# Attention with hashed buckets and a squared-ReLU block: the last key block of the softmax sums, and two small operations moved with it

## The chip, the cores and the metric

The kernel runs on one core of one Trainium2 chip. The metric is the device time of one execution in microseconds (us). It was timed three times before the change: 906.41, 908.99 and 909.02, so the median is 908.99 us. The profiled execution is another one; it counted 907.58 us, and its profile spans 905.8 us.

## The reference

There are 4 x 8 heads of 768 tokens and 64 features. Each token gets a 6-bit bucket number from the signs of a small projection, and a query attends only to the keys of its own bucket. The result goes, head by head, side by side, into a two-layer block with a squared ReLU.

```python
q_bits = (np.einsum('bhsd,dk->bhsk', q, proj) > 0)     # and k_bits
mask = q_bucket[:, :, :, None] == k_bucket[:, :, None, :]
scores = np.where(mask, scale * q @ k.T, -1e9)
attn = np.exp(scores - max); attn = attn / (attn.sum(-1, keepdims=True) + 1e-09)
x = attn @ v                                           # to (3072, 512)
h = np.maximum(x @ w_in, 0.0)                          # (3072, 2048)
out = (h * h) @ w_out                                  # (3072, 512)
```

Above, the lines are shortened: `@` stands for the batched products. The part that the change touches is the sum `attn.sum(-1)` of the exponentials over the keys, its reciprocal, and the preparation of the key bits.

## The kernel before, in words

The kernel has two stages. In the first one (up to about 345 us) attention is done for 16 pairs of heads, one turn of the loop over `pr` each; the second one does the two dense layers. The order of all instructions in the first stage is written out by hand: each engine runs its own instructions in the order in which the code issues them, and an instruction waits by semaphores for what it reads and for the buffers that it overwrites.

One turn of the loop over `pr` does these things. The keys are cut into six blocks of 128 (`SB` is 6). `score` (L375) makes the scores of one key block against all 768 queries of both heads, transposed, so that keys lie on the partitions. It does so in two pieces, of 512 and 256 queries, with two kinds of matmul into the same sum (L385). The first multiplies bits (bf16), which adds a huge negative number where the buckets differ; the second multiplies features (fp32). ScalarE takes the exponential (L389) into `e`, one of four ring buffers, which are used in turn. The score tiles take turns in three PSUM slots, which `hash` and `tot` (below) use too.

`attend` (L406) multiplies the exponentials of a key block with the values, into `xo`. The sum over the keys has two parts. Within a partition, `add_up` (L395) has VectorE add the exponentials of one key block after another to `total`, 128 x 1536 numbers each time; it is called for blocks 1 to 4 and starts with blocks 0 and 1 together. Across partitions, and with the sixth block (number 5), `sum_up` (L422) has TensorE multiply both `total` and the sixth block's `e` with a matrix of ones, 128 x 32, into `tot` (L430): for each of the two sources one matmul per head and half of the queries, each into 32 of the 128 partitions of `tot`. The four of one source thus use the four column tiles of TensorE. An fp32 matmul appears as two in the profile, so L430 has sixteen per turn. VectorE then transposes `tot` (`flip`, L436), adds a tiny constant (L438), takes the reciprocal (L442) and spreads it over two halves (`both`, L444). `spread` (L450) has TensorE distribute this over the partitions, and `normalize` (L461) multiplies `xo` with it and stores the result.

Pairs overlap. In turn `pr`, after the first two scores, `finish(pr - 1)` does the hash matmuls for pair `pr + 1` (`prepare`: `hash_bits`, L337, and then `signs` on ScalarE, L347, eight of them), then `sum_up`, the last two `attend` and `spread` of pair `pr - 1`. `features` (L321) transposes queries and keys of the next pair on VectorE. `weigh` (L368) multiplies the key bits of the next pair, 128 x 768 in bf16, by a factor per partition (`gains`); it is a VectorE instruction (L371), issued after the first `add_up` and before `normalize`, and in the first turn after block 3's `add_up`.

Between these the loop prepares the dense layers' weights, which arrive as float64: `load_weight` (L121, on SP's queue), `part_weight` (L134, VectorE, L141 and L145), `place_power` (L151, ScalarE, L158 and L159) and `round_weight` (L161, VectorE, L169 to L177), two pieces a turn. In six turns (pairs 4, 5, 8, 9, 10 and 11; the dictionary `sums`, L510) VectorE also makes sums of weights or of activations at the end of the turn (`sums_in`, L495, and `sums_x`, L534).

## Time and profile before

| | |
|---|---|
| Median of three runs | 908.99 us |
| Span of the profiled execution | 905.8 us |
| VectorE adds L402 | 64, median 1752 ns |
| TensorE L430, both sources | 256 matmuls, medians 498 and 486 ns |
| VectorE factor L371 | 15, median 414 ns |
| VectorE constant L438 | 16, median 173 ns |
| ScalarE exponentials L389 | 192, 591 to 1034 ns |

The page of the profile has the busy time of each engine, the span in 40 slices (here about 22.6 us each), the DMA queues, the chain of waits, and the costliest groups of instructions. The engines are PE (TensorE), PEld (its weight loads), DVE (VectorE), ACT (ScalarE), POOL (GpSimd) and SP (SyncE). The chain of waits is followed back from the last instruction of the execution: at each step to what released it, or to the instruction before it on its engine. The slices show how full the engines are along the span; attention takes the first fifteen.

```profile
PE   8999999999999999999999999999999999999994
...
DVE  5788899798998885887777776677778666777874
ACT  5878878887788761222211112221111122221110
```

A digit is the busy share in tenths; TensorE's row counts as busy also where matmuls overlap each other. In a timeline, a row gives start, length, engine, line, operation, tiles, sizes and count, and in brackets how long the engine was idle before it and what ended that. Since matmuls overlap, the length of a row is not what it moves TensorE on by; the start of the next row tells that.

### The profile page before, as it was taken

How to read it: one execution, taken by the hardware profiler on the slowest of the kernel's cores; microseconds unless marked ns; L12 is line 12 of the kernel's file. 1: busy time of each engine (PE TensorE's matmuls, PEld its weight loads, DVE VectorE, ACT ScalarE, POOL GpSimd, SP SyncE). 2: the span in 40 equal slices, each digit the busy share in tenths (PEclk: the TensorE clock that was granted, in tenths of full speed). 3: DMA queues.
4: the chain of work that ended last, by engine and by line, in shares of the span. 5: the costliest groups of instructions: out<-in, count | busy, mean ns of one | idle time of the engine just before them, and what ended most of it. 6: DMA issues, size and time to landing. Idle time of an engine off the chain costs nothing.

```text
span 905.8 us, 11897 instructions
## 1 busy us (share of the span) xinstructions
PE 884.4 (98%) x4372; PEld 504.5 (56%) x4372; DVE 697.6 (77%) x1012; ACT 363.4 (40%) x593; POOL 91.4 (10%) x149
## 2 busy tenths in 40 slices
PE   8999999999999999999999999999999999999994
PEld 3444444444444444443688854445888644458884
DVE  5788899798998885887777776677778666777874
ACT  5878878887788761222211112221111122221110
POOL 2000000000000000564000011112000211100002
PEclk9999999999999999999999999999999999999998
DMA  9577769778977326999765735557757455545575
GB/s 180 107 146 139 198 175 204 172 251 210 233 182 162 112 99 185 279 273 287 253 219 159 178 67 151 152 151 221 278 150 183 75 151 152 149 130 159 144 188 82
DMA packets 253407, 158.14 MB, mean 175 GB/s; under 512 B 166496, under 2 KB 215648, under 8 KB 253344
## 3 DMA queue, kind: packets, MB, share of 16 engines
q1 hardware_dynamic: 218448, 84.04, 39.4%
q10 hardware_dynamic: 24160, 37.89, 14.4%
q0 software_dynamic: 10736, 35.40, 12.8%
q8 instruction: 36, 0.59, 0.3%
q14 instruction: 27, 0.22, 0.1%
HBM read 119.28 MB, written 38.01 MB: 174 GB/s over the span
## 4 chain that ended last, share of the span: by engine, by line
PE 93%; DMA 3%; DVE 2%; ACT 1%; issue 1%; ACTq 0%; DVEq 0%
PE acc L675 57%; PE st L385 17%; PE xo L412 14%; PE tot L430 3%; PE hash L337 2%; DMA w_unit<-w_in 2%; DMA k_nat<-in_k_dram 1%; ACT bits L347 1%; ACT e L389 0%; DVE peaks L716 0%; DVE b L765 0%; DMA out_dram<-ot 0%; DMA leaf<-w_out 0%; DVE h L764 0%; DVE t L491 0%
## 5 line engine op out<-in xcount | busy, mean ns | idle before, releaser
L389 ACT ACTIVATE e<-st 128x1024 f32<-128x1024 f32 x192 | 145.2, 810 | 67.7 <-PE st L385 62.7
L675 PE MATMUL acc<-x,w_unit 128*128 128x512 f32 x384 | 169.6, 593 | 1.8 <-DMA w_unit<-w_in 1.8
L385 PE MATMUL st<-feat,feat 64*128 64x512 f32 (+1 forms) x768 | 150.4, 483 | 0.0
L412 PE MATMUL xo<-e,v_nat 128*64 128x512 f32 (+1 forms) x768 | 134.8, 492 | 0.0
L675 PE MATMUL acc<-b,leaf 128*128 128x256 f32 x600 | 133.0, 379 | 0.0
L675 PE MATMUL acc<-t_x,w_unit 128*128 128x512 f32 x288 | 127.8, 593 | 0.0
L675 PEld LDWEIGHTS acc<-x,w_unit 128*128 128x128 f32 x384 | 72.8, 190 | 92.7 <-issue 89.2
L675 PEld LDWEIGHTS acc<-b,leaf 128*128 128x128 f32 x600 | 113.8, 190 | 17.1 <-issue 1.7
L412 PEld LDWEIGHTS xo<-e,v_nat 128*64 128x64 f32 x768 | 51.4, 136 | 82.4 <-issue 70.3
L675 PEld LDWEIGHTS acc<-t_x,w_unit 128*128 128x128 f32 x288 | 54.5, 190 | 69.8 <-issue 67.7
L385 PEld LDWEIGHTS st<-feat,feat 64*128 64x128 f32 x768 | 66.1, 188 | 34.9 <-issue 26.8
L402 DVE TENSOR_TENSOR total<-total,e 128x1536 f32<-128x1536 f32 x48 | 84.2, 1753 | 1.7
L764 DVE TENSOR_TENSOR h<-acc,two 128x512 f32<-128x512 f32 x24 | 16.6, 691 | 86.2 <-PE acc L675 86.2
L675 PE MATMUL acc<-t,leaf 128*128 128x256 f32 x336 | 76.6, 380 | 0.8 <-ACT one L682 0.4
L682 ACT COPY two<-acc 128x512 f32<-128x512 f32 (+1 forms) x45 | 21.9, 486 | 131.8 <-PE acc L675 113.3
L347 ACT ACTIVATE bits<-hash,lifts 32x384 bf16<-32x384 f32 x124 | 70.9, 572 | 7.1 <-issue 3.5
L675 PEld LDWEIGHTS acc<-t,leaf 128*128 128x128 f32 x336 | 63.6, 190 | 10.5 <-DVE t L491 1.1
L682 ACT COPY one<-acc 128x512 f32<-128x512 f32 (+1 forms) x45 | 21.9, 486 | 117.0 <-PE acc L675 75.2
L765 DVE SCALAR_TENSOR_TENSOR b<-h 128x512 f32<-128x512 f32 x96 | 64.2, 690 | 2.5
L385 PE MATMUL st<-bits,bits 64*128 64x256 bf16 (+1 forms) x384 | 63.2, 325 | 2.4 <-ACT e L389 1.2
L675 PE MATMUL acc<-b_t,leaf 128*128 128x256 f32 x240 | 54.2, 380 | 1.3 <-issue 1.3
L675 PEld LDWEIGHTS acc<-b_t,leaf 128*128 128x128 f32 x240 | 45.4, 190 | 8.1 <-issue 2.0
(125 smaller groups left out, 871.4 us busy)
## 6 DMA issues: line engine op xcount, KB each, us to landing
leaf<-w_out ACTq DMA_DIRECT2D x142, 256.0 KB, 3.0
w_unit<-w_in SPq DMA_DIRECT2D x24, 896.0 KB, 6.0
raw<-in_moe_w_in_dram SPq DMA_DIRECT2D x16, 512.0 KB, 5.5
raw<-in_moe_w_out_dram SPq DMA_DIRECT2D x16, 512.0 KB, 4.7
w_out<-sums POOLq DMA_DIRECT2D x16, 448.0 KB, 7.0
v_nat<-in_v_dram SPq DMA_DIRECT2D x16, 384.0 KB, 4.9
x_all<-x_t SPq DMA_DIRECT2D x16, 384.0 KB, 3.1
x<-x_all POOLq DMA_DIRECT2D x3, 2048.0 KB, 13.0
```

The source lines that it names most:

```text
L337: nc.tensor.matmul(out=banks[g * NR_B:(g + 1) * NR_B, h, 0:HS], lhsT=projs[rows], rhs=feat[pr, w][rows, c * HS:(c + 1) * HS], start=True, ...
L347: nc.scalar.activation(out=t[h * D:h * D + NR_B, c * HS:(c + 1) * HS], in_=hashed[pr, w][at, h, 0:HS], func=ACTF.Sign, scale=HUGE, bias=li ...
L385: nc.tensor.matmul(out=st[:, h, 0:hi - lo], lhsT=src[pr, 1][rows, key], rhs=src[pr, 0][rows, lo:hi], start=first, stop=not first,)
L389: nc.scalar.activation(out=e[:, :, lo:hi], in_=st[:, :, 0:hi - lo], func=ACTF.Exp, scale=scale)
L402: nc.vector.tensor_tensor(out=totals[pr], in0=in0, in1=weights[pr, kt][:, :, 0:S], op=ALU.add)
L412: nc.tensor.matmul(out=xo[h * D:(h + 1) * D, lo:hi], lhsT=nat[pr, "v_nat"][:, h, kt * D:(kt + 1) * D], rhs=weights[pr, kt][:, h, lo:hi], s ...
L430: nc.tensor.matmul(out=tot[g * 32:(g + 1) * 32, 0:HS], lhsT=ones, rhs=src[:, h, c * HS:(c + 1) * HS], start=src is totals[pr], stop=src is ...
L675: nc.tensor.matmul(out=acc[to], lhsT=a(i), rhs=b(i), start=first and i == 0, stop=last and i == n - 1, skip_group_check=True,)
L682: nc.scalar.copy(out=t, in_=acc[of])
L764: nc.vector.tensor_tensor(out=h, in0=one, in1=two, op=ALU.add)
L765: nc.vector.scalar_tensor_tensor(out=out[:, r], in0=h, scalar=0.0, in1=h, op0=ALU.max, op1=ALU.mult)
```

## The change

It has five parts, all in the first stage.

- `add_up` is also called for the sixth key block (number 5), at the end of the turn, in the ten turns whose pair is not in `sums`. In those, `sum_up` multiplies only `total` with the ones; in the other six pairs it still multiplies both sources.
- The first add of a pair becomes an operation with a scalar, which adds the tiny constant `SB * TINY` to the sum of blocks 0 and 1 on each partition.
- For that, the add of the constant `S * TINY` after the flip (L438) goes; the reciprocal reads the flip itself.
- `weigh` becomes a ScalarE activation (Copy with a factor per partition) in place of the VectorE multiplication.
- `weigh` is issued elsewhere: after the scores of blocks 2 and 3 and ahead of `place_power(a)`, and in the first turn after the scores of blocks 4 and 5 and ahead of `place_power(b)`.

```diff
     def weigh(pr):
 
         t = bits[pr, 1]
-        nc.vector.tensor_scalar(out=t, in0=t, scalar1=gains, scalar2=None, op0=ALU.mult)
+        nc.scalar.activation(out=t, in_=t, func=ACTF.Copy, scale=gains)
...
     def add_up(pr, kt):
 
-        if kt == 0 or kt == SB - 1:
-            return
         if kt == 1:
             totals[pr] = p_n.tile([P, 2, S], FP32, name="total")
-        in0 = weights[pr, 0][:, :, 0:S] if kt == 1 else totals[pr]
-        nc.vector.tensor_tensor(
-            out=totals[pr], in0=in0, in1=weights[pr, kt][:, :, 0:S], op=ALU.add
-        )
+            nc.vector.scalar_tensor_tensor(
+                out=totals[pr], in0=weights[pr, 0][:, :, 0:S], scalar=SB * TINY,
+                in1=weights[pr, 1][:, :, 0:S], op0=ALU.add, op1=ALU.add,
+            )
+        else:
+            nc.vector.tensor_tensor(
+                out=totals[pr], in0=totals[pr], in1=weights[pr, kt][:, :, 0:S], op=ALU.add
+            )
...
         tot = tot[:, 0]
-        for src in (totals[pr], weights[pr, SB - 1]):
+        srcs = [totals[pr]] + [weights[pr, SB - 1]] * (pr in sums)
+        for src in srcs:
             for c in range(2):
                 for h in range(2):
                     g = 2 * h + c
                     nc.tensor.matmul(
                         out=tot[g * 32:(g + 1) * 32, 0:HS], lhsT=ones,
                         rhs=src[:, h, c * HS:(c + 1) * HS],
-                        start=src is totals[pr], stop=src is not totals[pr],
+                        start=src is srcs[0], stop=src is srcs[-1],
                     )
         flip = p_n.tile([P, HS], FP32, name="flip")
         nc.vector.transpose(out=flip, in_=tot[:, 0:HS])
         once = p_n.tile([P, NB], FP32, name="once")
-        nc.vector.tensor_scalar(
-            out=once, in0=flip.rearrange("p (n f) -> p n f", f=32)[:, :, 0],
-            scalar1=S * TINY, scalar2=None, op0=ALU.add,
+        nc.vector.reciprocal(
+            out=once, in_=flip.rearrange("p (n f) -> p n f", f=32)[:, :, 0]
         )
-        nc.vector.reciprocal(out=once, in_=once)
...
-            elif more:
-                weigh(pr + 1)
             if pr > 0:
                 normalize(pr - 1)
...
             if pr == 0:
                 prepare()
+            elif more:
+                weigh(pr + 1)
             place_power(a)
...
-            if pr == 0:
-                weigh(1)
...
             score(pr, 5)
+            if pr == 0:
+                weigh(1)
             place_power(b)
             attend(pr, 2)
             attend(pr, 3)
             add_up(pr, 4)
+
+            if pr not in sums:
+                add_up(pr, 5)
             if pr in sums:
```

## The prediction

> **What bounds the kernel now.** I read the page first (engines, then the chain of waits), to see whose work sets the end.

> ```profile
> PE 884.4 (98%) x4372; PEld 504.5 (56%) x4372; DVE 697.6 (77%) x1012; ACT 363.4 (40%) x593; POOL 91.4 (10%) x149
> ...
> PE 93%; DMA 3%; DVE 2%; ACT 1%; issue 1%; ACTq 0%; DVEq 0%
> PE acc L675 57%; PE st L385 17%; PE xo L412 14%; PE tot L430 3%; PE hash L337 2%; DMA w_unit<-w_in 2%; DMA k_nat<-in_k_dram 1%; ACT bits L347 1%; ACT e L389 0%; DVE peaks L716 0%; DVE b L765 0%; DMA out_dram<-ot 0%; DMA leaf<-w_out 0%; DVE h L764 0%; DVE t L491 0%
> ```

> TensorE holds 93% of the chain, in the attention (up to about 345 us) as in the dense part. The change touches attention alone, and of the chain there only `tot L430`. So what matters is whether TensorE can really start the next thing earlier once half of L430 is gone. For that I took the timeline of the turn that starts at 113.9 us.

> ```profile
> 117.24 0.88 PE L337 MATMUL hash<-feat,projs 64*32 64x384 f32 x16
> ...
> 118.05 0.85 PE L430 MATMUL tot<-total,ones 128*32 128x384 f32 x8
> ...
> 118.36 4.68 ACT L347 ACTIVATE bits<-hash,lifts 32x384 bf16<-32x384 f32 x8
> ...
> 118.72 0.83 PE L430 MATMUL tot<-e,ones 128*32 128x384 f32 x8
> ...
> 119.47 2.81 PE L412 MATMUL xo<-e,v_nat 128*64 128x512 f32 x16
> ...
> 119.61 0.58 DVE L436 STREAM_TRANSPOSE flip<-tot 128x384 f32<-128x384 f32 x1 [0.69 <-PE tot L430]
> ...
> 120.23 0.17 DVE L438 TENSOR_SCALAR once<-flip 128x12 f32<-128x12 f32 x1
> ...
> 122.47 0.41 DVE L371 TENSOR_SCALAR bits<-bits,gains 128x768 bf16<-128x768 bf16 x1
> ...
> 123.92 0.38 PE L385 MATMUL st<-bits,bits 64*128 64x512 bf16 x2
> ...
> 126.75 0.72 ACT L158 ACTIVATE small<-power,excess 128x512 uint8<-128x512 uint32 x1
> ...
> 127.50 0.63 ACT L159 ACTIVATE power<-small 128x512 uint32<-128x512 uint8 x1
> ...
> 129.67 3.13 ACT L389 ACTIVATE e<-st 128x1024 f32<-128x1024 f32 x4 [1.54 <-PE st L385]
> ```

> TensorE goes from one row to the next without a hole; VectorE and ScalarE wait for it (0.69 and 1.54 us). The first `tot` start of one turn lies 20.55 us before that of the next in nearly every turn. The windows tell how full the two others are, one turn without weight sums (60 to 81 us) and one with them (101 to 122):

> ```profile
> 60.00:81.00 21.00, 21.00 (x162) 9.68 (x160) 17.47 (x24) 16.68 (x26) 0.00 (x0) 1.00 0.66 126
> ...
> 101.00:122.00 21.00, 21.00 (x162) 9.64 (x160) 19.96 (x28) 16.68 (x26) 0.00 (x0) 1.00 0.62 160
> ```

> Columns: PE, PEld, DVE and ACT busy, with instruction counts. VectorE has 3.5 us free in 21 in the first and 1.0 in the second; ScalarE 4.3 in both. The sums-free turns are the ten that get the sixth add.

> [...] L402 has a median of 1752 ns. [...] in L430 each matmul takes 0.49 us, yet eight of them move TensorE on by only 118.72 - 118.05 = 0.67 us.

> **The change part by part.**

> *Sums on TensorE, removed in ten turns.* Four products of two matmuls each go. They are not worth 8 x 0.49 us but what TensorE moves on: groups of four (one per column tile) start at 118.05, 118.39, 118.72 and 119.05, then the attend at 119.47. The step from the last group to the attend stays; two groups at 0.33 go, 0.66 us. The chain of waits gives 1.43 us for sixteen, 0.71 for half; I take 0.66.

> *The sixth add on VectorE, ten times 1.75 us.* The adds for which it runs are the sums-free pairs 0 to 3, 6, 7 and 12 to 15. It stands after the fifth add and ahead of the next `features` (two transposes, 0.97 and 0.94 us), whose results hash needs, and of `round_weight` (three at 0.69), ahead of the flip. In the turn shown the four sums of the weights stand in that very place, 4 x 0.63 = 2.5 us start to start, and hash was in time (k-features ended 117.02, its second half started about 117.6). 1.75 is less than 2.5, so features and flip come no later than here. VectorE's load in a sums-free turn becomes 17.1 (17.47 x 20.55/21) + 1.75 - 0.41 - 0.17 = 18.3 us of 19.9: hidden, with 1.6 to spare. In the last pair it isn't hidden: its fifth add starts at 337.87, the sixth could start at 339.54 and end at 341.29, where `tot` started at 341.04. That is 0.3 us of delay, and 0.35 of the 0.66 is left.

> *The key factor to ScalarE, 15 times.* Off VectorE: 0.41 us. On ScalarE: the trace has no such row. L158 with 256 elements more, at the 0.85 ns an element between the 512 and 1024 exponentials (593 and 1027 ns), gives 0.94 us[...]. Bounds 0.85 (L159 alike) and 1.0; I take 0.93. It stands after the exponential of block 3 and before L158. Behind it are L158 and L159 and then the exponential at 129.67, and who waits for those is `round_weight` on VectorE and the score slots on TensorE. From 126.75, 0.93 + 1.38 ends at 129.1: under 129.67, so the 1.54 us idle hides it. `round_weight` (128.94 before) comes some 0.2 us late, less than what VectorE has gained by then (0.41 + 0.17). In the first turn the factor stands after the exponential of block 5, which ended at 30.14; ready by about 31.1, needed by the next turn's first score at 31.69. The added wait of ScalarE on its own signs costs nothing, as these are done by then.

> *The constant with the first sum.* Two-tensor operation with a scalar: 0.69 us for 512 elements (L177) against 0.68 for the plain add (L485), so 1.75 again; upper bound 1.85 from L471 (1.02 at 768, reading PSUM). The 0.17 us of L438 go from the path flip, once, spread, which was hidden behind the 2.81 us attend. SP's and POOL's queues keep their order.

> *Sum.* 9 x 0.66 + 0.35 = 6.3 us, from 905.8 (this profile's span) to 899.5. That execution counted 907.58, and the three timed ones 906.41 to 909.02. Off the median of 908.99: 902.7.

> **The rivals.**

> *ScalarE's signs hold TensorE (gain 1.5 to 4 us, 905 to 907.5).* The third score tile of a turn (123.92) takes the PSUM slot of `hash`, free when the eight signs end at 118.36 + 4.68 = 123.04. These follow hash, not `tot`, so they don't move up. TensorE would now ask at 123.26. A release takes about 0.05 us where the trace shows one (signs ended at 25.79, score at 25.84), so 0.17 us is left. For: the margin is thin, and the exponential behind the signs must follow closely. Against: it suffices by these rows. It touches the eight shortened turns that have signs.

> *The gain is given back at a transfer (gain about 2.3 us, 906.7).* In one later turn VectorE waited for weights:

> ```profile
> 215.13 0.43 DVE L141 TENSOR_SCALAR power<-raw 128x512 uint32<-128x512 uint32 x1 [1.96 <-DMA raw<-in_moe_w_out_dram]
> ```

> That turn took 22.41 instead of 20.55 us. Six shortened turns lie before it; were the landing fixed in time, 6 x 0.66 = 4.0 would go. Against: its requests are issued by the same loop after x is stored, and at 184 to 192 us the DMA is nearly idle, so it moves along.

> *Slower: VectorE becomes the bound of the ten turns (912).* If its waits inside a turn (for exponentials, placed powers, `tot`) come to more than the 1.6 us to spare, each turn lags, and the features make hash late. With 1 us lag a turn, nine times 1.0 - 0.66 = +3 us. For: VectorE is at 95% in sums turns. Against: these run at 20.55 with more work on it. It decides only from a sixth add dearer than about 3.3 us.

> **How the numbers follow.** Forecast 0.68, signs 0.13, transfer 0.11, VectorE 0.08. About 0.3% (2.7 us) is what a measurement of this kernel can tell from no change. The forecast is faster but for a few hundredths, two thirds of the signs case and a third of the transfer case too: faster 0.79, same 0.13, slower 0.08. Range: the forecast with the spread of the runs before (906.4 - 6.3 = 900.1, less 0.4 for 0.71 instead of 0.66) gives 899.7 below; above, the signs case down to a gain of 2.6 us, 906.4.

> **What would show it.** Right: `tot` with 176 matmuls instead of 256, 1.75 us adds 74 instead of 64; start to start of `tot` about 19.9 us in the shortened turns; L371 on ScalarE at 0.93 us with no new wait of TensorE. Wrong: TensorE waiting in `st` for `bits L347`, or in hash for `feat`; VectorE no longer waiting at the flip; the wait at the weights of that one turn grown by more than a microsecond; L371 above 1.6 us.

## The result, and the profile after

The changed kernel took 900.88 us (median of six, 899.60 to 905.62), the kernel before beside it 908.04 us (906.41 to 909.02). The ratio is 0.9932, with a 95% interval of 0.9906 to 0.9957: faster by 0.7%, or 7.2 us. The forecast was 902.7 us, a gain of 6.3 from the 908.99 us of the first three runs before; 1 us of the difference between 902.7 and 900.88 is that the kernel before has a median of 908.04 us here.

The profile is of the slowest of these six executions: it counted 905.62 us and spans 903.8. TensorE's granted clock was halved once in its dense stage (0.50 from 412.78 to 419.60 us), which the last section takes up; so the whole span can't be set against the 905.8 before. The attention stage has the full clock in both (1.00). The first matmul of the dense stage starts at 345.29 us before and at 337.62 after: attention lost 7.67 us. A second profile of the changed kernel (run `after_again`, below) has 337.86, in a span of 898.4.

From the page of the changed kernel, engines and the head of the chain of waits:

```profile
PE 880.1 (97%) x4292; PEld 503.7 (56%) x4292; DVE 711.4 (79%) x991; ACT 376.0 (42%) x608; POOL 91.7 (10%) x149
...
PE 88%; DMA 5%; DVE 4%; ACT 1%; issue 1%; ACTq 0%; SPq 0%; DVEq 0%
```

TensorE has 80 matmuls fewer, and VectorE 13.8 us more work. A shortened turn, in the timeline after (the lines that answer to those shown before; L433 is the old L430, L414 the old L412, L439 the old L436; L404 are the adds, of which the second at 88.72 is the sixth, and L324 the features behind it):

```profile
75.00 0.88 PE L337 MATMUL hash<-feat,projs 64*32 64x384 f32 x16
...
75.80 0.85 PE L433 MATMUL tot<-total,ones 128*32 128x384 f32 x8
76.12 4.68 ACT L347 ACTIVATE bits<-hash,lifts 32x384 bf16<-32x384 f32 x8
76.59 2.81 PE L414 MATMUL xo<-e,v_nat 128*64 128x512 f32 x16
76.72 0.58 DVE L439 STREAM_TRANSPOSE flip<-tot 128x384 f32<-128x384 f32 x1 [0.65 <-PE tot L433]
...
81.04 0.38 PE L385 MATMUL st<-bits,bits 64*128 64x512 bf16 x2
...
83.86 0.94 ACT L371 ACTIVATE bits<-bits,gains 128x768 bf16<-128x768 bf16 x1
84.71 0.71 ACT L158 ACTIVATE small<-power,excess 128x512 uint8<-128x512 uint32 x1
85.44 0.63 ACT L159 ACTIVATE power<-small 128x512 uint32<-128x512 uint8 x1
...
86.78 3.13 ACT L389 ACTIVATE e<-st 128x1024 f32<-128x1024 f32 x4 [0.71 <-PE st L385]
...
88.72 3.61 DVE L404 TENSOR_TENSOR total<-total,e 128x1536 f32<-128x1536 f32 x2
...
93.14 0.93 DVE L324 STREAM_TRANSPOSE feat<-k_nat 128x768 f32<-128x768 f32 x1
```

From `tot` to the attend it is now 0.79 us (75.80 to 76.59), where it was 1.42. TensorE waits for nothing here: the features that hash needs end at 94.07 us, and the next hash starts at 94.90. ScalarE, with the factor in its queue, waits 0.71 us for the scores instead of 1.54. VectorE still waits for TensorE at the flip, 0.65 us. The 0.69 us in the turn shown of before are no measure for this, as that turn has weight sums: in the turns without sums VectorE waited 3.2 us there. That wait has paid for the sixth add. All waits at the flip between 40 us and the end of attention, before and after (in total, how often, the longest):

```profile
DVE flip L436 <- PE tot L430: 33.0, 15, 3.2
```

```profile
DVE flip L439 <- PE tot L433: 11.3, 15, 1.6
```

The stretch from 60 to 81 us, which before had 17.47 us of VectorE and 16.68 of ScalarE:

```profile
60.00:81.00 21.00, 21.00 (x158) 9.66 (x156) 19.62 (x24) 18.13 (x28) 0.00 (x0) 1.00 0.69 126
```

The distances between the first `tot` starts of successive turns tell what each turn takes (us; "to 1" is from the `tot` of pair 0 to that of pair 1):

| | to 1, 2, 3, 4 | to 5, 6 | to 7, 8 | to 9 | to 10, 11, 12 | to 13 | to 14 | to 15 | then to the dense stage |
|---|---|---|---|---|---|---|---|---|---|
| before | 20.55 each | 20.55 each | 20.55 each | 22.41 | 20.55 each | 20.55 | 19.75 | 16.41 | 4.25 |
| after | 19.91 each | 20.55 each | 19.91 each | 20.55 | 20.55 each | 19.91 | 19.10 | 16.26 | 3.60 |

Each distance contains the `tot` of the pair that it starts from. Nine of the ten shortened ones give 0.64 or 0.65 us. Pair 14's, in the column "to 15", gives only 0.15, as TensorE has to wait 0.43 us ahead of the last `tot`. The turn "to 9" lost 1.86 us that no part of the change was forecast to touch: the wait for the weights is gone. The start-up takes 0.15 us more (0.39 in `after_again`).

### The profile page after: what moved, and what is told of

Same layout as the page of the kernel before. It is cut to its first block, busy times and chain, and to the rows that moved or that the text cites. A ratio compares the mean times of both kernels' runs of the same rounds, so it can differ in the third digit from the quotient of the medians.

```text
span 903.8 us, 11749 instructions
## 1 busy us (share of the span) xinstructions
PE 880.1 (97%) x4292; PEld 503.7 (56%) x4292; DVE 711.4 (79%) x991; ACT 376.0 (42%) x608; POOL 91.7 (10%) x149
## 4 chain that ended last, share of the span: by engine, by line
PE 88%; DMA 5%; DVE 4%; ACT 1%; issue 1%; ACTq 0%; SPq 0%; DVEq 0%
PE acc L679 54%; PE st L385 17%; PE xo L414 14%; DMA w_unit<-w_in 3%; PE tot L433 2%; PE hash L337 2%; DMA out_dram<-ot 1%; DVE total L404 1%; DMA k_nat<-in_k_dram 1%; ACT bits L347 1%; DVE peaks L720 0%; DVE ot L834 0%; DVE b L769 0%; ACTq L809 0%; ACT e L389 0%
## 5 line engine op out<-in xcount | busy, mean ns | idle before, releaser
L679 PE MATMUL acc<-x,w_unit 128*128 128x512 f32 x384 | 172.2, 600 | 4.2 <-DMA w_unit<-w_in 4.2
L389 ACT ACTIVATE e<-st 128x1024 f32<-128x1024 f32 x192 | 145.2, 810 | 50.1 <-PE st L385 45.6
L385 PE MATMUL st<-feat,feat 64*128 64x512 f32 (+1 forms) x768 | 150.4, 483 | 0.0
L414 PE MATMUL xo<-e,v_nat 128*64 128x512 f32 (+1 forms) x768 | 134.8, 492 | 0.0
L679 PE MATMUL acc<-b,leaf 128*128 128x256 f32 x600 | 132.9, 379 | 0.0
L679 PE MATMUL acc<-t_x,w_unit 128*128 128x512 f32 x288 | 127.8, 593 | 0.5 <-ACT one L686 0.5
L679 PEld LDWEIGHTS acc<-x,w_unit 128*128 128x128 f32 x384 | 73.8, 193 | 96.8 <-issue 90.6
L679 PEld LDWEIGHTS acc<-b,leaf 128*128 128x128 f32 x600 | 114.0, 190 | 16.8 <-issue 1.4
L404 DVE TENSOR_TENSOR total<-total,e 128x1536 f32<-128x1536 f32 x58 | 101.9, 1757 | 3.8
L414 PEld LDWEIGHTS xo<-e,v_nat 128*64 128x64 f32 x768 | 51.3, 136 | 82.4 <-issue 75.0
L679 PEld LDWEIGHTS acc<-t_x,w_unit 128*128 128x128 f32 x288 | 54.5, 190 | 70.2 <-issue 67.7
L385 PEld LDWEIGHTS st<-feat,feat 64*128 64x128 f32 x768 | 66.1, 188 | 33.9 <-issue 25.2
L679 PE MATMUL acc<-t,leaf 128*128 128x256 f32 x336 | 76.6, 380 | 0.7 <-ACT one L686 0.4
L347 ACT ACTIVATE bits<-hash,lifts 32x384 bf16<-32x384 f32 x124 | 71.0, 573 | 4.9 <-PE hash L337 1.6
L679 PEld LDWEIGHTS acc<-t,leaf 128*128 128x128 f32 x336 | 63.6, 190 | 10.5 <-DVE t L492 1.1
L385 PE MATMUL st<-bits,bits 64*128 64x256 bf16 (+1 forms) x384 | 63.2, 325 | 2.4 <-ACT e L389 1.2
L679 PE MATMUL acc<-b_t,leaf 128*128 128x256 f32 x240 | 54.2, 380 | 2.0 <-issue 2.0
L679 PEld LDWEIGHTS acc<-b_t,leaf 128*128 128x128 f32 x240 | 45.4, 190 | 8.8 <-issue 2.7
```

The lines of the kernel that those rows point to most:

```text
L347: nc.scalar.activation(out=t[h * D:h * D + NR_B, c * HS:(c + 1) * HS], in_=hashed[pr, w][at, h, 0:HS], func=ACTF.Sign, scale=HUGE, bias=li ...
L385: nc.tensor.matmul(out=st[:, h, 0:hi - lo], lhsT=src[pr, 1][rows, key], rhs=src[pr, 0][rows, lo:hi], start=first, stop=not first,)
L389: nc.scalar.activation(out=e[:, :, lo:hi], in_=st[:, :, 0:hi - lo], func=ACTF.Exp, scale=scale)
L404: nc.vector.tensor_tensor(out=totals[pr], in0=totals[pr], in1=weights[pr, kt][:, :, 0:S], op=ALU.add)
L414: nc.tensor.matmul(out=xo[h * D:(h + 1) * D, lo:hi], lhsT=nat[pr, "v_nat"][:, h, kt * D:(kt + 1) * D], rhs=weights[pr, kt][:, h, lo:hi], s ...
L679: nc.tensor.matmul(out=acc[to], lhsT=a(i), rhs=b(i), start=first and i == 0, stop=last and i == n - 1, skip_group_check=True,)
```

## The experiments

**Which part does what.** Two kernels with one half of the change each. `sixth_only` leaves the factor and the constant as they were before:

```diff
-        if kt == 0 or kt == SB - 1:
+        if kt == 0:
             return
...
-        for src in (totals[pr], weights[pr, SB - 1]):
+        srcs = [totals[pr]] + [weights[pr, SB - 1]] * (pr in sums)
+        for src in srcs:
...
             add_up(pr, 4)
+            if pr not in sums:
+                add_up(pr, 5)
```

> Only the sixth add of the ten pairs and the dropped second source; the key factor stays on VectorE in its old place and the small constant stays after the flip. My theory (TensorE moves up by what it no longer does, VectorE has room): the shortened turns take 19.9 us, attention loses 6.2 us, and the whole is 902 us beside 908. If the stall of 1.9 us in the turn after the weight wait is tied to how early x is stored, it stays here. Rival (VectorE needs the relief by the two small moves): without it the features make hash late in the shortened turns, TensorE waits there for VectorE, and less than half of the gain, under 3 us, is left (905 or more).

Measured: 900.83 us (six executions, 898.42 to 903.54), ratio 0.9933 (0.9913 to 0.9953). Shortened turns 19.91 us, the turn "to 9" 21.72, and attention ends at 338.99. The rival falls: VectorE keeps up without the relief. By the times, the sixth add alone gives the whole gain (900.83 and 900.88 us); what the small moves add to it shows in the traces alone. `small_only` is the changed kernel without the sixth add:

```diff
-        srcs = [totals[pr]] + [weights[pr, SB - 1]] * (pr in sums)
+        srcs = [totals[pr]] + [weights[pr, SB - 1]]
...
-            if pr not in sums:
-                add_up(pr, 5)
```

> Only the two small moves: key factor on ScalarE, constant with the first sum; both sources still go through TensorE in all pairs. My theory: TensorE's work per turn is untouched, so turns stay at 20.55 us. If the vanished 1.9 us stall after the weight wait came from x being stored about 1 us earlier in a turn, as VectorE no longer does the factor ahead of it, it is gone here too: 906 us. If its vanishing was the luck of one execution, or needs the shortened turns, the time is that of before, 908. Rival (ScalarE was short of time): TensorE waits for exponentials or signs, over 909.

Measured: median 906.30 beside 907.20, but a ratio of 1.0001 (0.9987 to 1.0014), so no difference in time that can be told; its executions spread from 904.78 to 912.54. In the trace the turns take what they took before, but for "to 9" with 20.74, and attention ends at 343.97. The two halves add up: against 345.05 us (the mean of two profiles of the kernel before) 6.1 and 1.1 us, together 7.2; both together gave 7.2 to 7.4.

> The kernel before once more, for a second profile. If the weight wait (about 2 us) and the stall after it (1.9 us) are the kernel's own, both are there again, and the attention ends near 345.3 us. If they were the luck of one execution, it ends near 343.4 us. 907 to 909 us either way.

Measured: 906.19 us, the wait for weights 1.5 us, "to 9" 21.93, attention until 344.80. So wait and stall are the kernel's own. The same place, VectorE's L141 in the turn of pair 9, in the timelines of `sixth_only`, of `small_only` and of the changed kernel:

```profile
210.92 0.43 DVE L141 TENSOR_SCALAR power<-raw 128x512 uint32<-128x512 uint32 x1 [1.27 <-DMA raw<-in_moe_w_out_dram]
```

```profile
213.82 0.43 DVE L141 TENSOR_SCALAR power<-raw 128x512 uint32<-128x512 uint32 x1 [0.23 <-DMA raw<-in_moe_w_out_dram]
```

```profile
209.42 0.42 DVE L141 TENSOR_SCALAR power<-raw 128x512 uint32<-128x512 uint32 x1
```

From 1.96 (and 1.5) through 1.27 and 0.23 to nothing: the small moves take most of the wait away, the sixth add a part of it. What goes with it is when x is stored. The normalized x of pair 7 was ready 6.8 us after that turn's `tot` began before (186.49 - 179.71), 6.1 in `sixth_only`, 6.4 in `small_only` and 5.8 in the changed kernel. The load of x into the dense stage (2048 KB) waits for that store. While it was under way and shortly after (before, it was issued at 191.31 and landed at 201.50), SP's queue, which also asks for the weights, moved slowly: the four loads of q from 198.29 took 6.42 us to issue, and 2.52 in the next turn. Behind them the request for the weights was issued 29.3 us after that `tot` before (29.0 in `before_again`), 27.7 in `small_only`, 26.6 in `sixth_only` and 26.1 in the changed kernel. That the earlier store is the cause was argued from this order, not tried by itself; and it isn't the whole cause, as in `sixth_only` the transfer took 7.4 us to land and in the others 5.2 to 6.1.

**Where VectorE becomes the bound.** The sixth add in all sixteen pairs:

```diff
-        srcs = [totals[pr]] + [weights[pr, SB - 1]] * (pr in sums)
+        srcs = [totals[pr]]
...
-            if pr not in sums:
-                add_up(pr, 5)
+            add_up(pr, 5)
```

> The sixth add in all sixteen pairs, so TensorE multiplies one source only in every pair. My theory: in the six turns with weight or activation sums VectorE has 19.5 - 0.6 + 1.75 = 20.7 us of work for a turn that TensorE could do in 19.9; VectorE becomes the bound there, hash waits for features, those turns take about 20.7 to 21 us instead of 20.55, and the time is 1 to 3 us above that of the changed kernel (902 to 904). Rival (TensorE alone counts): six more turns shorten by 0.65, 897 us.

Measured: 905.87 us (ratio 0.9986, 0.9978 to 0.9995), 5 us above the changed kernel; the direction was right, the size short. The six turns take 21.4 to 21.6 us. The timeline of one of them, in `all_sixteen`:

```profile
108.82 3.61 DVE L404 TENSOR_TENSOR total<-total,e 128x1536 f32<-128x1536 f32 x2
...
112.36 0.68 DVE L486 TENSOR_TENSOR s_in<-in 128x512 f32<-128x512 f32 x1
...
114.88 0.97 DVE L324 STREAM_TRANSPOSE feat<-q_nat 128x768 f32<-128x768 f32 x1
...
115.78 0.94 DVE L324 STREAM_TRANSPOSE feat<-k_nat 128x768 f32<-128x768 f32 x1
116.00 1.62 PE L337 MATMUL hash<-feat,projs 64*32 64x384 f32 x16 [0.92 <-DVE feat L324]
```

The fifth and sixth add, the sums and the features now stand in one row; hash waits 0.92 us for the first half and runs 1.62 instead of 0.88 us, as its second half waits too. This is the slower rival of the prediction, on the chip: not in the ten turns where it was feared, but in the six that the change leaves out.

How near are the ten? `half_add_more` puts an add of 128 x 768 into a spare tile behind each of their sixth adds:

```diff
             if pr not in sums:
                 add_up(pr, 5)
+                extra(pr)    # nc.vector.tensor_tensor(out=spare, in0=..., in1=..., op=ALU.add)
```

The comment stands for the body of `extra`, shortened.

> The changed kernel with half an add more (0.9 us on VectorE, into a spare tile) behind each sixth add. By the prediction, VectorE has 1.6 us to spare in such a turn, so nothing changes: 901. By the run with the sixth add in all pairs, a turn bound by VectorE takes its 20.7 us of work and 0.9 us of waits that it can't avoid; then the spare is only about 0.7 us, the shortened turns take 20.1 to 20.2 us instead of 19.9, and the time is some 2 us higher, 903.

Measured: 902.29 us beside 901.13 of the changed kernel in the same series. The added row takes 0.95 us:

```profile
73.56 0.95 DVE L410 TENSOR_TENSOR spare<-e 128x768 f32<-128x768 f32 x1
```

It moves the next row by 0.87 (74.43 - 73.56), and the shortened turns grow from 19.91 to 19.97 us. So 0.8 us is to spare in each, half of the 1.6 reckoned and near the other theory's 0.7, though that theory's turns of 20.1 to 20.2 us were too long. VectorE's wait at the flip is 0.00 us in seven of these ten turns: the spare is used up. The times of the two kernels overlap, and the trace is what tells them apart. The start-up takes the larger part of the loss: the first `tot` starts 0.9 us later (37.15 for 36.23).

**Where ScalarE becomes the bound.** One more sign behind the eighth, so that hash's slot is freed later:

```diff
+                if w == 0 and pr > 1 and c == 1 and h == 1:
+                    nc.scalar.activation(out=spare[...], in_=hashed[pr, w][at, h, 0:HS], ...)
```

> The changed kernel with one more activation (0.57 us) behind the eighth sign of each turn, reading the same slot into a spare tile, so that the slot is freed 0.57 us later. By the prediction's margin of 0.17 us, TensorE now waits 0.4 us for the slot in the shortened turns that have signs: +3 us, about 904, with turns of 20.3. If the margin was in truth larger (0.6 or more), nothing changes: 901.

Measured: 902.92 us, 1.8 above the changed kernel, and attention ends 2.2 us later than in `after_again`; shortened turns with signs take 20.20 us (the first of them 20.02). The timelines of `signs_late`, TensorE and then ScalarE:

```profile
61.79 0.39 PE L391 MATMUL st<-bits,bits 64*128 64x512 bf16 x2
```

```profile
61.19 0.56 ACT L353 ACTIVATE spare<-hash,lifts 32x384 bf16<-32x384 f32 x1
61.77 1.51 ACT L395 ACTIVATE e<-st 128x1024 f32<-128x1024 f32 x2
```

The third score tile starts 0.04 us after the added sign has ended: the slot decides, as the rival said. In the changed kernel it starts at 81.04 and the signs end at 76.12 + 4.68 = 80.80, so with the same 0.04 us for the release 0.20 us is left. The added sign moved the end by 0.47 (it overlaps the eighth), and 0.47 - 0.20 = 0.27 is what each turn lost, within 0.02.

**Is there more to have?** If VectorE's load makes the six turns long, another engine could take their sums. `pool_sums` is `all_sixteen` with the weight and activation sums of attention on GpSimd (one line of several):

```diff
-        nc.vector.tensor_tensor(out=s1, in0=a21, in1=a22, op=ALU.add)
+        on.tensor_tensor(out=s1, in0=a21, in1=a22, op=ALU.add)      # on: nc.gpsimd in attention
```

> The sixth add in all sixteen pairs, with the weight and activation sums of the attention's six turns given to GpSimd, which does little there. Theory (VectorE's load makes the six turns long): VectorE now has the load of a shortened turn everywhere, all turns take 19.9 us, and the time is 3.9 us below the changed kernel, 897. Rival: GpSimd's adds slow VectorE's, or come so late that the stores behind them hold up the next loads; then the six turns stay above 20.5 us and the time is 901 or more.

Measured: 910.91 us, ratio 1.0035 (1.0022 to 1.0047): slower than before the change. Most turns do take 19.91 us, but three take 22.66 to 26.68 and one 20.30. The timelines of `pool_sums` in the first of these (24.74), VectorE and then GpSimd:

```profile
103.29 1.49 DVE L145 TENSOR_SCALAR top<-raw 128x512 uint32<-128x512 uint32 x1
104.70 5.57 DVE L404 TENSOR_TENSOR total<-total,e 128x1536 f32<-128x1536 f32 x2
110.19 1.75 DVE L169 SCALAR_TENSOR_TENSOR power<-raw,power 128x512 uint32<-128x512 uint32 x1
111.86 0.68 DVE L174 SCALAR_TENSOR_TENSOR top<-raw,top 128x512 f32<-128x512 uint32 x1
```

```profile
103.05 1.45 POOL L487 TENSOR_TENSOR s_in<-in 128x512 f32<-128x512 f32 x1
104.46 1.45 POOL L488 TENSOR_TENSOR s_in<-in 128x512 f32<-128x512 f32 x1
105.87 2.78 POOL L489 TENSOR_TENSOR s_in<-s_in,in 128x512 f32<-128x512 f32 x1
108.73 2.66 POOL L490 TENSOR_TENSOR s_in<-in,s_in 128x512 f32<-128x512 f32 x1
```

While GpSimd adds, VectorE's two adds take 5.57 us instead of 3.6, L169 1.75 instead of 0.69 and L145 1.49 instead of 0.42; L174, after GpSimd's end at 111.4, takes 0.68 again. The adds and L169 read two tiles each, L145 one, so in this trace operations of both kinds were slowed; what the two engines contend for isn't shown. GpSimd doesn't keep to the turns: it makes the sums of two turns, eight operations, in one row from 96.4 to 111.4, so that they fall on one turn's work of VectorE. In this turn TensorE then waited 1.39 us for exponentials and 1.80 for features, and its clock was at half for 3.4 us from 118.14. The rival holds.

`sums_last` moves only the sums of activations, on VectorE, from the turns of pairs 10 and 11 to the last one, and gives these two pairs the sixth add:

```diff
-    for n in range(2):
-        sums[X_0 + 1 + n] = lambda n: sums_x(0, n), n
...
                 add_up(pr, 5)
+            if not more:
+                sums_x(0, 0)
...
         finish(NP - 1)
+        sums_x(0, 1)
```

> The changed kernel with the sums of activations (four operations of 1.2 us) moved from the turns of pairs 10 and 11 to the last turn, where VectorE waits 1.0 us at the flip and 1.7 us before the last normalization; pairs 10 and 11 get the sixth add too. Theory: two more turns shorten from 20.55 to 19.91 us (-1.3 us), and the last turn loses at most half a microsecond: 900 us beside 901, attention ending near 337 us. Rival: the moved sums make the dense stage's first matmuls wait, and its first sums on VectorE come 2 us late; then nothing is gained, 901 or more.

Measured: 900.37 us, ratio 0.9919 (0.9904 to 0.9935), which can't be told from the changed kernel's in the series before. In the trace the two turns take 19.91 us and attention ends at 336.66, 1.2 us before `after_again`. The step is right in the trace and too small for the times; it isn't shown to beat the changed kernel.

> The changed kernel once more, for a second profile and beside the kernels of this series. If the 4.2 us in which TensorE waits for the weights of the dense stage at 414 us, and the half clock of 6.8 us that stands there in the first profile, belong to the change, both are here again and the span is above 902. If they come and go from one execution to the next, most executions stay near 900 to 901 and a few near 905, and the attention ends at 337.6 us either way.

Measured: 901.13 us (900.14 to 902.63), ratio 0.9919 (0.9904 to 0.9935); the profile is without half clock in the dense stage, until its last microseconds. So the long wait isn't in every execution of the changed kernel; whether the change makes it more frequent isn't shown.

## Why the prediction was right, point by point

*The sums on TensorE.* Right: 0.66 us forecast for each, 0.64 to 0.65 measured in nine turns. What decided was to count what TensorE moves on by, and not the 0.49 us of a matmul.

*The sixth add on VectorE.* Hidden, as forecast, and at the forecast price: L404 has a median of 1758 ns. The argument from its place (it is shorter than the weight sums that stand there in other turns) held. The load was reckoned at 18.3 us a turn and is 18.6 (19.62 x 19.91/21). Mis-sized was the spare: 1.6 us forecast, 0.8 measured by `half_add_more`. All of a turn's free time was counted as spare, though only a part of it is the wait for TensorE at the flip: from 60.85 to 80.76 us of the changed kernel VectorE is busy for 18.56 of 19.91 us, and of the other 1.35 the flip's wait is 0.65. That wait would have told it better, and it could have been forecast: the wait at the flip was 3.2 us in a like turn before; less 1.7 for the add, from start to start, and 0.66 for the earlier `tot`, that leaves 0.8 to 0.9 (an estimate). The prediction read the flip in a turn with weight sums, where the wait is 0.69. In the last pair the delay was put at 0.3 us and is 0.43; only 0.15 us of the 0.66 is left there, where 0.35 was forecast:

```profile
334.02 0.85 PE L433 MATMUL tot<-total,ones 128*32 128x384 f32 x8 [0.43 <-DVE total L404]
```

*The factor on ScalarE.* 0.93 us forecast, a median of 0.935 measured, inside ScalarE's idle time; `round_weight` waits 0.2 us for its power in seven cases, as forecast.

*The constant.* Free, as forecast: L399 has a median of 1751 ns, that of the plain add before.

*The rivals.* The signs' margin was put at 0.17 us and is 0.20; it held. VectorE as the bound is real, but from 0.8 us more of work, and in the six turns that the change leaves out. The transfer rival had the sign wrong: the landing neither stayed nor only moved along with the loop, it came early enough that the wait ended. That is the step of the prediction that failed, "so it moves along", and it brought 1.9 us against the first profile of before and 1.4 against the second. The reading under it was wrong too: from 184 to 192 us the DMA isn't nearly idle, its mean share is 0.44 (about 1 from 188 to 190), and from 192 to 204, with the load of x, it is 0.94.

*The sum.* What the forecast had counted brought 5.95 us of its 6.3: nine times 0.64 to 0.65, and 0.15 in the last pair. The weight turn brought 1.86 more, and the start-up took 0.15 back: the 7.67 us of the first two profiles. In the second two they are 1.38 and 0.39, together 6.94. So about a fifth of the gain is luck as far as the forecast goes: its own terms came out nearly as forecast, and this part it had ruled out.

## What to carry to other kernels

Where an engine packs several small operations side by side, price the removal of some by the distance between starts, not by their durations (here eight matmuls of 0.49 us each gave 0.64 to 0.65 us a turn). An add may be moved to another engine where it takes the place of longer work in a like turn (here 1.75 us where other turns have 2.5 us of weight sums); but the room there is the wait that this engine has for the bound one, not its idle share (here 0.65 us of wait and 0.8 of room by `half_add_more`, where the idle time had given 1.6). And before handing adds to GpSimd, look at what VectorE is doing at that moment: in `pool_sums` two of its adds took 5.57 us beside GpSimd's, and 3.6 without.

## What the runs showed that had not been expected

TensorE waits for the weights of the dense stage's next unit at some 410 to 423 us in every profile. How long it waits differs, and the clock with it. The same window of the first profile of the changed kernel and of `after_again` (the number before the last two is the granted clock, as a share of the full one):

```profile
412.00:420.00 8.00, 5.78 (x8) 2.44 (x9) 6.93 (x9) 0.59 (x1) 5.35 (x7) 0.57 0.98 302
```

```profile
412.00:420.00 8.00, 8.00 (x19) 3.54 (x20) 7.89 (x11) 1.76 (x3) 5.12 (x7) 1.00 0.98 294
```

The waits were 4.23 and 1.59 us. After 4.23 us (2.99 in `all_sixteen`, and 3.76 in one long turn of `pool_sums`) the clock was at half for 6.8 us. TensorE worked in 5.4 of them, so about 2.7 us were lost beside the wait (an estimate, half of 5.4; L679's matmuls, 0.59 us at their median, took up to 1.22 there). Waits of 0.94 to 1.90 us at that place brought no half clock, in nine profiles. But in `sums_last` a wait of 1.89 us at 703.8 us had a half clock of 3.4 us with it, and one of 2.16 us at 706.4 in `half_add_more` had none. So the length of a wait alone does not decide.

Further, in `pool_sums` GpSimd's add of 128 x 512 took 1.27 us at its shortest and up to 2.88 beside VectorE's work.
